# A fused attention and gated-MLP block: attention in 64x32 TensorE tiles, six score banks in turn, and one double exponential in each pair

## The chip, the cores and the metric

The kernel runs on one core of one Trainium2 chip as a single program. The core has a matrix engine (TensorE, PE below; its weight loads are PEld), a vector engine (DVE), an activation engine (ACT), a general engine (POOL) and a queue processor that issues transfers (SP). The metric is the device time of one execution in microseconds (us). Matmul results land in an accumulator memory of eight banks, each holding 128 x 512 single-precision numbers; ACT and DVE read them there. An engine takes its instructions in the order in which they stand in the program, and an instruction that needs another engine's result waits for a counter of that engine to reach a number.

## The reference, cut to what matters

```python
x = A_x                                         # [1, 2048, 512]
qkv = layernorm(x) @ wqkv                       # 32 heads of 16 columns
scores = einsum("bhqd,bhkd->bhqk", q, k) * 16 ** -0.5
p = softmax(scores); o = einsum("bhqk,bhkd->bhqd", p, v)
h = x + o @ wo
z = gelu(layernorm(h) @ w_in)                   # 1376 columns, halves z1 and z2
g = w_sp @ layernorm(z2) + b_sp[:, None]        # mixes the 2048 rows
out = h + (z1 * g) @ w_out
```

The softmax subtracts each row's maximum, so the kernel needs for each head and each of 2048 queries a bound over 2048 keys, then exp(score - bound) for all 32 x 2048 x 2048 scores, and the weighted sum of values.

## The kernel before, in words

Three stages follow each other: projections (up to about 160 us), attention (to about 1293 us), and the output projection with the gated MLP. The change lies in attention, and the rest is told only where attention meets it.

**Tiling.** Heads go in eight groups of four. Within a group the two heads t = 0 and t = 1 of a product pair sit in rows 0 to 49 and 64 to 113 of PE's array, and p = 0 or 1 chooses the pair. Queries go in four blocks of 512, keys in sixteen blocks of 128. A unit is (head group, query block, key block); the main loop takes two units, a *pair* of key blocks kb and kb1, at a time, 256 pairs in all. The split of queries and keys into half-precision parts makes the contraction 48 rows, and two rows more carry the row's bound.

**Scores and exponentials** (`score`, `product`). For each pair PE makes eight score blocks s0 to s7, each 128 keys x 512 queries with one matmul (L805) of 50 rows x 128 columns. ACT reads each from its bank and writes its exponential to a tile `pt` (L814). Three banks, three separate tiles called `s`, go round.

**Maxima for a later query block** (`max_pair`). The loop also works ahead on the bounds of a query block some pairs later. In each pair PE makes eight more products `m` (L223): seven end in a DVE pass over 128 x 512 (six `reduce_max`, L228, and one two-operand pass, L237), and one is read by ACT as an absolute value (L233) that the two-operand pass combines. Four banks, four separate tiles m0 to m3, go round. The first eleven of the 256 maxima steps run ahead of the main loop; the other 245 stand one in each of the first 245 pairs. One pair follows without maxima, and ten pairs in which a 128 x 1024 exponential over two banks takes two scores at once (`scores2`, L823), beside first matmuls of the output projection (`make_h`, L747).

**Weighted values** (`weigh`, L830). `pt` is the single-precision moving operand and 32 columns of values, one of them ones, are the stationary one: 128 rows x 32 columns, four such matmuls j = 0 to 3 side by side in the four column strips, added up in one bank `pv` over sixteen key blocks. Each is carried out as two matmul instructions. After the last key block DVE copies `pv` to `og` (`take`, L840) and two DMAs send it off; the sums come back by DMA and are inverted (`invert`, L777).

**What sets the order.** The string `PAIR` is written out by hand: the tokens s, M, H (half of the previous block's weighing), P (the whole of this block's) are emitted one after another onto the engines' queues. POOL works through a list of chores that prepare later weights, with a budget in each pair. Waits are not written in the kernel: the layer that records it sets them from the tiles that each instruction writes and reads.

Of the kernel before, what the change touches and what calls it, by code (L numbers as in the profile page):

```python
# [8 lines left out]
F32 = mybir.dt.float32  # L9
# [13 lines left out]
H = 32  # L23
# [16 lines left out]
PAIR = "s0 M0 join s2 M4 M1 s1 H s3 invert M2 s5 M3 H out M5 s4 M7 turn s6 s7 M6 P".split()  # L40
# [19 lines left out]
def block_kernel(ctx: ExitStack, tc: tile.TileContext, x, wqkv, wo, w_in, w_sp4, b_sp, w_out, out):  # L60
# [144 lines left out]
    def max_pair(m):  # L205
# [14 lines left out]
        def scores(t, keys, b):  # L220
            r = slice(RG * t, RG * t + KS)
            acc = bank(b)
            nc.tensor.matmul(acc, q[r, p, c], keys[r, p], start=True, stop=True)  # L223
            return acc

        def one(t, e, b):
            acc = scores(t, k[:, :, 512 * e:512 * e + 512], b)
            nc.vector.reduce_max(at(t, e if t else e - 1), acc, axis=AX.X)  # L228

        def minus(b):  # L230
# [4 lines left out]
        def plus(b):  # L235
# [15 lines left out]
        four = [lambda b, e=e: one(1, e, b) for e in range(4)]  # L251
        two = [lambda b, e=e: one(0, e, b) for e in (2, 3)]
# [535 lines left out]
    with ExitStack() as at:  # L788
# [4 lines left out]
        pp = at.enter_context(tc.tile_pool(name="pp", bufs=6))  # L793
        ps_v = at.enter_context(tc.tile_pool(name="ps_v", bufs=1, space=PSUM))
        inner = at.enter_context(ExitStack())
        ps_m3 = inner.enter_context(tc.tile_pool(name="ps_m3", bufs=1, space=PSUM))
        ps_s = inner.enter_context(tc.tile_pool(name="ps_s", bufs=3, space=PSUM))
        more.clear()
        more[3] = lambda: ps_m3.tile([P, 512], F32, name="m3")
        pv = {}  # L800

        def product(s, hg, qb, kb, p, t):

            r = slice(RG * t, RG * t + KM)
            nc.tensor.matmul(s, kst[hg % 2][r, p, kb * P:(kb + 1) * P],  # L805
                             qst[hg * NQ + qb][r, p, :], start=True, stop=True)

        def score(hg, qb, kb, p, t):
# [3 lines left out]
            s = ps_s.tile([P, 512], F32, name="s")  # L812
            product(s, hg, qb, kb, p, t)
            nc.scalar.activation(pts[p, kb][:, t, :], s, AF.Exp, scale=scales_[hg // 2])  # L814

        def scores2(hg, qb, kb, p):

            pts[p, kb] = pp.tile([P, 2, 512], F32, name="pt")
            turn[0] += 1
            s = later[turn[0] % 3 != 1].tile([P, 2, 512], F32, name="s2")  # L820
# [4 lines left out]
        def weigh(hg, qb, kb, a=0, b=512):  # L825
            if kb == 0:
                pv[0] = ps_v.tile([P, 512], F32, name="pv")
            for j in range(4):
                c = (4 * kb + j) * VW
                nc.tensor.matmul(pv[0][32 * j:32 * j + 32, a:b], vst[hg % 2][:, c:c + 32],  # L830
                                 pts[j % 2, kb][:, j // 2, a:b], start=kb == 0, stop=kb == NB - 1,
                                 skip_group_check=True)
            if b == 512:
                for p in range(2):
                    del pts[p, kb]

        def take(hg, qb, pool=sm):

            o = pool.tile([P, 512], F32, name="og", bufs=2)
            nc.vector.tensor_copy(o, pv[0])  # L840
# [204 lines left out]
        for n in range(0, len(units), 2):  # L1045
# [15 lines left out]
            steps = max_pair(m) if m < 8 * HG * NQ else []  # L1061
            m += 1
            if not steps and not later:
                maxima.close()
                later.append(attn.enter_context(
                    tc.tile_pool(name="ps_l", bufs=1, space=PSUM, side="right")))
                steps_h.append(make_h(h_rows[0], later[0].tile([P, 512], F32, name="h")))
            elif not steps and len(later) == 1:
                inner.close()
                later.append(at.enter_context(tc.tile_pool(name="ps_t", bufs=2, space=PSUM)))  # L1070
# [13 lines left out]
            if len(later) == 2:  # L1084
                if turned:
                    max_rows()
                more_h = n in (492, 494, 508, 510)
                scores2(hg, qb, kb, 0)
                scores2(hg, qb, kb, 1)
                some_h(1 + more_h)  # L1090
                weigh(*prev)
                if ends:
                    take(*prev[:2])
                scores2(hg, qb, kb1, 0)
                scores2(hg, qb, kb1, 1)
                some_h(1)
                weigh(hg, qb, kb)
            first = True
            for tok in PAIR if len(later) < 2 else ():
# [504 lines left out]
```

## Time and profile before

| what | value |
|---|---|
| median of 3 runs | 1713.79 us (1713.14 to 1713.97) |
| profiled execution, its span | 1712.3 us |
| median less that span | 1.5 us (the profiled execution's own time is not listed; the span and this remainder stand for it) |
| first exponential of attention | starts at 160.66 us |
| last of the 40 double exponentials | ends at 1292.5 us |
| granted PE clock, mean | 1.000 |

The page gives for each engine its busy time, that time's share of the span and its number of instructions; its slice lines give the busy share in 40 equal slices of 42.8 us, so attention fills slices 4 to 30. A group's mean duration is from the start of an instruction to its end; ACT and DVE start the next one before the end of the last, so the sum of durations can exceed the time taken. Rows of the timeline give start, duration, engine, line, operands and a count, with the idle time before it in square brackets and what ended it.

### The profile page before, as it was taken

Reading aid. Unit: us, or ns where it says so; the run is one execution under the profiler, and the core shown is the slowest. Engines: PE = TensorE matmul, PEld = TensorE weight load, DVE = VectorE, ACT = ScalarE, POOL = GpSimd, SP = SyncE. Lnnn points to the kernel's source line nnn. Section 1 sums busy time; section 2 is a strip of 40 time slices with the busy share of each in tenths; the row PEclk is TensorE's granted clock in tenths of the full one; section 3 lists DMA queues with packets and bytes.
Section 4 is the critical chain, followed back from the end, with each engine's and each line's share of the span. In section 5 each row is a group of like instructions: output and inputs, shape, how many; then the busy total and the mean of one; then the engine's idle time right before and its main releaser. Section 6 shows DMA issues by size and latency. Waiting matters only on the chain.

```text
span 1712.3 us, 36689 instructions
## 1 busy us (share of the span) xinstructions
PE 1699.5 (99%) x13508; PEld 644.7 (38%) x13508; DVE 1452.5 (85%) x3051; ACT 1317.5 (77%) x2584; POOL 813.6 (48%) x1062
## 2 busy tenths in 40 slices
PE   9999999999999999999999999999999999999999
PEld 4533222222222222222222222222225666656665
DVE  7688999999999999999999999999936787543444
ACT  4334999999999999999999999999995545211111
POOL 1231867776673267687767776400002766300100
PEclk9999999999999999999999999999999999999999
DMA  5534332342221244344434444300114454664551
GB/s 185 167 94 144 103 89 68 101 94 82 81 68 25 56 118 117 104 144 125 130 113 124 132 140 130 80 13 19 37 39 124 140 173 140 233 234 156 198 217 44
DMA packets 189309, 196.03 MB, mean 114 GB/s; under 512 B 67496, under 2 KB 140008, under 8 KB 189128
## 3 DMA queue, kind: packets, MB, share of 16 engines
q1 hardware_dynamic: 186824, 188.04, 36.8%
q10 hardware_dynamic: 2304, 5.64, 0.8%
q8 instruction: 106, 1.74, 0.4%
q14 instruction: 75, 0.61, 0.1%
HBM read 122.10 MB, written 65.93 MB: 110 GB/s over the span
## 4 chain that ended last, share of the span: by engine, by line
PE 78%; DVE 12%; DMA 3%; POOL 2%; ACT 2%; SPq 2%; issue 1%; ACTq 0%; POOLq 0%; DVEq 0%
PE pv L830 26%; PE s L805 17%; PE m L223 9%; DVE mx L228 7%; PE acc L107 4%; PE g L108 4%; PE g L109 4%; PE g L107 4%; PE acc L109 4%; PE acc L108 4%; DMA rc<-r_scr 1%; DVE ab L237 1%; DVE og L840 1%; SPq L723 1%; DVE rs_t L124 1%
## 5 line engine op out<-in xcount | busy, mean ns | idle before, releaser
L814 ACT ACTIVATE pt<-s 128x512 f32<-128x512 f32 x1968 | 1006.2, 637 | 5.5 <-PE m L223 4.3
L228 DVE TENSOR_REDUCE mx<-m 128x1 f32<-128x512 f32 x1510 | 947.5, 682 | 11.7 <-PE m L223 2.9
L805 PE MATMUL s<-qst,kst 50*128 50x512 f16 x2048 | 604.2, 379 | 0.2
L830 PE MATMUL pv<-pt,vst 128*32 128x256 f32 (+1 forms) x6056 | 598.1, 466 | 4.1 <-DVE og L840 1.3
L223 PE MATMUL m<-kst,qst 48*128 48x512 f16 x1510 | 452.4, 381 | 0.0
L805 PEld LDWEIGHTS <-kst 50*128 50x128 f16 x2048 | 132.0, 94 | 352.1 <-issue 323.7
L830 PEld LDWEIGHTS pv<-pt,vst 128*32 128x32 f32 x6056 | 119.5, 108 | 290.7 <-issue 277.3
L223 PEld LDWEIGHTS <-qst 48*128 48x128 f16 x2048 | 159.2, 93 | 173.6 <-issue 124.2
L223 PE MATMUL m<-uvs,qst 48*128 48x512 f16 x504 | 190.5, 380 | 0.6 <-DVE mx L228 0.6
L245 POOL TENSOR_SCALAR nm<-nm 128x16 f32<-128x16 f32 x32 | 6.6, 206 | 358.8 <-DVE nm L242 358.8
L237 DVE CUSTOM_DVE_ANT_0 ab<-m,ab 128x512 f32<-128x512 f32 x252 | 170.5, 677 | 2.7 <-ACT ab L233 2.7
L233 ACT ACTIVATE ab<-m 128x512 f32<-128x512 f32 x252 | 157.3, 624 | 15.5 <-PE m L223 14.8
L1368 ACT ACTIVATE pr<-pr,up 128x304 f32<-128x304 f32 (+1 forms) x32 | 17.0, 574 | 109.2 <-DVE up L1322 109.2
L991 POOL TENSOR_TENSOR op<-raw,op 128x512 f16<-128x512 f32 x80 | 92.9, 1161 | 6.0
L914 POOL TENSOR_TENSOR raw<-raw 128x512 f32<-128x512 f32 (+1 forms) x84 | 83.3, 991 | 6.7
L919 POOL TENSOR_TENSOR acc_sp<-acc_sp,raw 128x512 f32<-128x512 f32 x63 | 80.4, 1277 | 4.5
L109 PE MATMUL acc<-wi,hT 128*128 128x344 f16 x256 | 79.1, 309 | 0.3 <-DVE hT L104 0.3
L107 PE MATMUL acc<-wi,hT 128*128 128x344 f16 x256 | 79.1, 309 | 0.0
L108 PE MATMUL acc<-wi,hT 128*128 128x344 f16 x256 | 79.1, 309 | 0.0
L1510 POOL TENSOR_TENSOR pr<-pr,z 128x344 f32<-128x344 f32 x8 | 7.3, 914 | 145.9 <-DMA whole<-squares 108.3
L911 POOL TENSOR_SCALAR raw<-raw 128x512 f32<-128x512 f32 (+1 forms) x88 | 52.3, 594 | 19.7 <-DMA raw<-in_wqkv 12.4
L1509 DVE TENSOR_TENSOR pr<-g,v 128x344 f32<-128x344 f32 x8 | 4.1, 517 | 66.6 <-PE g L109 63.5
(247 smaller groups left out, 2292.9 us busy)
## 6 DMA issues: line engine op xcount, KB each, us to landing
raw<-in_w_sp SPq DMA_DIRECT2D x128, 256.0 KB
s_scr<-op SPq DMA_DIRECT2D x64, 256.0 KB
op<-s_scr SPq DMA_DIRECT2D x32, 512.0 KB
a_scr<-op SPq DMA_DIRECT2D x48, 256.0 KB
op<-a_scr SPq DMA_DIRECT2D x24, 512.0 KB
o_scr<-og SPq DMA_DIRECT2D x64, 128.0 KB
qst<-q_scr SPq DMA_DIRECT2D x192, 32.0 KB
kst<-k_scr SPq DMA_DIRECT2D x48, 128.0 KB
```

What stands on the lines that cost most here:

```text
L107: nc.tensor.matmul(ps, lh, rh, start=first, stop=False, **kw)
L108: nc.tensor.matmul(ps, lh, rl, start=False, stop=False, **kw)
L109: nc.tensor.matmul(ps, ll, rh, start=False, stop=last, **kw)
L223: nc.tensor.matmul(acc, q[r, p, c], keys[r, p], start=True, stop=True)
L228: nc.vector.reduce_max(at(t, e if t else e - 1), acc, axis=AX.X)
L233: nc.scalar.activation(ab[0], acc, AF.Abs)
L237: nc.vector.tensor_tensor_reduce(ab[0], acc, ab[0], 0.5, LOW, ALU.add, ALU.max, at(0, 0))
L805: nc.tensor.matmul(s, kst[hg % 2][r, p, kb * P:(kb + 1) * P], qst[hg * NQ + qb][r, p, :], start=True, stop=True)
L814: nc.scalar.activation(pts[p, kb][:, t, :], s, AF.Exp, scale=scales_[hg // 2])
L830: nc.tensor.matmul(pv[0][32 * j:32 * j + 32, a:b], vst[hg % 2][:, c:c + 32], pts[j % 2, kb][:, j // 2, a:b], start=kb == 0, stop=kb == NB - 1,
L914: pool.tensor_mul(got[0] if n else acc, got[0], got[0])
L991: chores.append((lambda: pool.tensor_sub(t[0][:, 1], of(), t[0][:, 0]), TT))
```

## The change

All attention matmuls of the main loop become tiles of 64 array rows x 32 array columns. A score or maxima product, one matmul before, is four (`by_quarters`, L237), one for each strip of 32 columns, with the same 512 moving columns. The weighing is split by key half: t = 0 takes keys 0 to 63 on array rows 0 to 63 and t = 1 keys 64 to 127 on rows 64 to 127, in two banks pv0 and pv1, so each weighing has twice as many matmuls with half the rows; at the end ACT copies pv1 to a tile `half` (L892) and DVE adds pv0 to it (in place of its copy).

The three `s` banks and four `m` banks become six banks of one tile, `slots`, of 128 x 6 x 512; the class `Slots` hands out the least recently used bank, or two neighbours. Scores s5 and s4 of each pair ("w5 w4") go to two neighbouring banks and one 128 x 1024 exponential (L862) takes both; the other six stay single (L851). The order strings are new: N and n are the maxima products with a `reduce_max` of head t = 1 and t = 0, A the one read by ACT (L271), C the two-operand one (L275), Q and R a half's weighing of the previous and of this key block. The first pair of a query block has a string of its own. In the last ten pairs the double exponentials draw on `slots` too, and one bank is held for the output projection.

```diff
-PAIR = "s0 M0 join s2 M4 M1 s1 H s3 invert M2 s5 M3 H out M5 s4 M7 turn s6 s7 M6 P".split()
+PAIR = "s0 s1 n N s2 Q1 Q0 s3 s6 N Q0 Q1 n w5 w4 N R0 R1 A N turn R0 s7 C R1 rows".split()
+FIRST_PAIR = "s0 s1 n N n Q1 s2 Q1 half Q0 s3 Q0 out N s6 N A w5 w4 R1 R0 R1 C turn s7 R0 N".split()
+SLOTS = 6
+    class Slots:
+        def __init__(self, pool, n):
+            self.acc = pool.tile([P, n, 512], F32, name="slots")
+            self.used, self.now = [0] * n, 0
+        def one(self):
+            i = min(range(len(self.used)), key=self.used.__getitem__)
+            self.mark(i)
+            return self.acc[:, i, :]
+        def two(self):
+            i = min(range(0, len(self.used), 2), key=lambda i: max(self.used[i:i + 2]))
+            self.mark(i)
+            self.mark(i + 1)
+            return self.acc[:, i:i + 2, :]
+    def by_quarters(acc, left, right):
+        for c in range(4):
+            c = slice(32 * c, 32 * c + 32)
+            nc.tensor.matmul(acc[c], left[:, c], right, start=True, stop=True)
         def scores(t, keys, b):
             r = slice(RG * t, RG * t + KS)
-            acc = bank(b)
-            nc.tensor.matmul(acc, q[r, p, c], keys[r, p], start=True, stop=True)
+            if slots:
+                acc = slots.one()
+                by_quarters(acc, q[r, p, c], keys[r, p])
+            else:
+                acc = bank(b)
+                nc.tensor.matmul(acc, q[r, p, c], keys[r, p], start=True, stop=True)
-        ps_m3 = inner.enter_context(tc.tile_pool(name="ps_m3", bufs=1, space=PSUM))
-        ps_s = inner.enter_context(tc.tile_pool(name="ps_s", bufs=3, space=PSUM))
+        slots = Slots(at.enter_context(tc.tile_pool(name="ps_s", bufs=1, space=PSUM)), SLOTS)
         def product(s, hg, qb, kb, p, t):
             r = slice(RG * t, RG * t + KM)
-            nc.tensor.matmul(s, kst[hg % 2][r, p, kb * P:(kb + 1) * P],
-                             qst[hg * NQ + qb][r, p, :], start=True, stop=True)
+            by_quarters(s, kst[hg % 2][r, p, kb * P:(kb + 1) * P], qst[hg * NQ + qb][r, p, :])
         def score(hg, qb, kb, p, t):
-            s = ps_s.tile([P, 512], F32, name="s")
+            s = slots.one()
+        def half_scores2(hg, qb, kb, p, t):
+            if not wide:
+                pts[p, kb] = pp.tile([P, 2, 512], F32, name="pt")
+                wide.append(slots.two())
+                product(wide[0][:, t, :], hg, qb, kb, p, t)
+            else:
+                s = wide.pop()
+                product(s[:, t, :], hg, qb, kb, p, t)
+                nc.scalar.activation(pts[p, kb], s, AF.Exp, scale=scales_[hg // 2])
-        def weigh(hg, qb, kb, a=0, b=512):
+        def weigh(hg, qb, kb, t, cols=256):
+            r, c = slice(RG * t, RG * t + RG), slice(a, a + cols)
             for j in range(4):
-                nc.tensor.matmul(pv[0][32 * j:32 * j + 32, a:b], vst[hg % 2][:, c:c + 32],
-                                 pts[j % 2, kb][:, j // 2, a:b], start=kb == 0, stop=kb == NB - 1,
-                                 skip_group_check=True)
+                v = (4 * kb + j) * VW
+                nc.tensor.matmul(pv[t][32 * j:32 * j + 32, c], vst[hg % 2][r, v:v + 32],
+                                 pts[j % 2, kb][r, j // 2, c], start=kb == 0 and not a,
+                                 stop=kb == NB - 1 and a + cols == 512,
+                                 tile_position=(RG * t, 32 * j), skip_group_check=True)
         def take(hg, qb, pool=sm):
-            nc.vector.tensor_copy(o, pv[0])
+            nc.vector.tensor_add(o, pv[0], halves.pop())
```

How the instructions of a pair stand is shown at three places, in the middle of attention, with the counters that each waits for in brackets (an engine's name with `_49` is its counter; a wait that stands alone is shown with the instruction behind it).

PE before: one matmul for each product; `m` tiles carry a number, since each bank is a tile of its own.

```order
L805 LDWEIGHTS kst_158
L805 MATMUL s<-qst,kst_158 128x512 [waits Activation_49]
L223 LDWEIGHTS qst
L223 MATMUL m_18133<-kst_1849,qst 128x512 [waits DVE_49]
L805 LDWEIGHTS kst_158
L805 MATMUL s<-qst,kst_158 128x512 [waits Activation_49]
L223 LDWEIGHTS qst
L223 MATMUL m_18140<-uvs_1850,qst 128x512 [waits DVE_49]
L830 MATMUL pv<-pt,vst_156 32x256 x4
```

PE in the changed kernel: products are rows of four with their weight loads, all into `slots`; only the first of the four waits.

```order
L237 LDWEIGHTS qst
L237 MATMUL slots<-uvs_159,qst 32x512 [waits DVE_49]
L237 LDWEIGHTS qst
L237 MATMUL slots<-uvs_159,qst 32x512
L237 LDWEIGHTS qst
L237 MATMUL slots<-uvs_159,qst 32x512
L237 LDWEIGHTS qst
L237 MATMUL slots<-uvs_159,qst 32x512
L237 LDWEIGHTS kst_158
L237 MATMUL slots<-qst,kst_158 32x512 [waits Activation_49]
```

What moved: eight instructions stand where two stood. In the rows before, the number that a product waits for is that of the instruction that last read the product's own bank, four to eight reads of a score or a maximum back. In the changed rows it is, fifteen times in a pair, that of the exponential or DVE pass that stands directly ahead in the program, of whichever bank: the product of the first row here waits for the DVE pass of the product just ahead of it, though the two lie in different banks.

ACT before, two pairs and the absolute values between them:

```order
L814 ACTIVATE pt<-s 128x512 [waits PE_49] x8
L233 ACTIVATE ab<-m_9444 128x512 [waits PE_49]
L814 ACTIVATE pt<-s 128x512 [waits PE_49] x8
L233 ACTIVATE ab<-m_9528 128x512 [waits PE_49]
L814 ACTIVATE pt<-s 128x512 [waits PE_49] x8
```

ACT in the changed kernel, one pair and the beginning of the next:

```order
L862 ACTIVATE pt<-slots 128x1024 [waits DVE_49,PE_49,Activation_49]
L271 ACTIVATE ab<-slots 128x512 [waits DVE_49,PE_49]
L851 ACTIVATE pt<-slots 128x512 [waits DVE_49,PE_49] x2
L851 ACTIVATE pt<-slots 128x512 [waits PE_49]
L851 ACTIVATE pt<-slots 128x512 [waits DVE_49,PE_49,Activation_49]
L851 ACTIVATE pt<-slots 128x512 [waits PE_49]
L851 ACTIVATE pt<-slots 128x512 [waits PE_49,Activation_49]
L862 ACTIVATE pt<-slots 128x1024 [waits DVE_49,PE_49,Activation_49]
```

What moved: two of the eight exponentials are one of 1024 columns. Before, every read of a score waits for PE alone. Now most wait for DVE's counter as well, for the DVE pass directly ahead; `Activation_49` stands for a reused `pt` buffer, several pairs back.

DVE before, the passes of one pair (the reduction of 16 columns is the negation at a block's end):

```order
L228 TENSOR_REDUCE mx<-m_11872 128x1 [waits PE_49]
L242 TENSOR_REDUCE nm<-mx 128x16 [waits DVE_49]
L228 TENSOR_REDUCE mx<-m_11885 128x1 [waits PE_49]
L228 TENSOR_REDUCE mx<-m_11888 128x1 [waits PE_49]
L228 TENSOR_REDUCE mx<-m_11901 128x1 [waits PE_49]
L228 TENSOR_REDUCE mx<-m_11916 128x1 [waits PE_49]
L228 TENSOR_REDUCE mx<-m_11922 128x1 [waits PE_49]
```

DVE in the changed kernel, one pair:

```order
L266 TENSOR_REDUCE mx<-slots 128x1 [waits PE_49,Activation_49]
L266 TENSOR_REDUCE mx<-slots 128x1 [waits PE_49]
L266 TENSOR_REDUCE mx<-slots 128x1 [waits PE_49,Activation_49]
L266 TENSOR_REDUCE mx<-slots 128x1 [waits PE_49]
L266 TENSOR_REDUCE mx<-slots 128x1 [waits PE_49,Activation_49] x2
L275 ISA ab,mx<-slots,ab 128x512 [waits PE_49,Activation_49]
L275 ISA mx 128x1
```

What moved: the same seven passes in a pair, in another order. Before, a reduction waits for PE alone; now, wherever an ACT instruction stands between two passes in the program, the second waits for ACT's counter too, for that ACT instruction.

126 lines of the change are left out of this document (66 added, 60 removed).

## The prediction

> **What bounds the kernel now.** I read the page first, its engine line and its slices, for where time lies and which engines are full there.
>
> ```profile
> span 1712.3 us, 36689 instructions
> PE 1699.5 (99%) x13508; PEld 644.7 (38%) x13508; DVE 1452.5 (85%) x3051; ACT 1317.5 (77%) x2584; POOL 813.6 (48%) x1062
> ...
> DVE  7688999999999999999999999999936787543444
> ACT  4334999999999999999999999999995545211111
> ```
>
> The change touches attention alone, about 1,130 us of the span, where three engines are full at once. One stretch of it in the view by windows says so more exactly (length; busy time and count of PE, PEld, DVE, ACT, POOL; then PE's granted clock, DMA share and GB/s):
>
> ```profile
> 750.00:1000.00 250.00, 249.12 (x2256) 70.77 (x2254) 248.14 (x479) 249.79 (x509) 182.84 (x223) 1.00 0.44 128
> ```
>
> The pace comes from ACT's rows in the timeline. The absolute value L233 stands once in a pair; its 11th and its last stand here.
>
> ```profile
> 164.29 0.60 ACT L233 ACTIVATE ab<-m 128x512 f32<-128x512 f32 x1
> ...
> 1247.96 0.62 ACT L233 ACTIVATE ab<-m 128x512 f32<-128x512 f32 x1
> 1248.44 0.63 ACT L814 ACTIVATE pt<-s 128x512 f32<-128x512 f32 x1
> ```
>
> There are 244 steps between them: (1247.96 - 164.29) / 244 = **4.44 us for a pair**. In it ACT makes nine passes, DVE seven and PE sixteen products and two weighings, and all this lies side by side: nine ACT passes of 0.64 us and seven DVE passes of 0.68, with their products, would take far longer than 4.44 one after another. What allows it is that seven banks are filled and emptied independently.
>
> ```profile
> L814 ACT ACTIVATE pt<-s 128x512 f32<-128x512 f32 x1968 | 1006.2, 637 | 5.5 <-PE m L223 4.3
> L228 DVE TENSOR_REDUCE mx<-m 128x1 f32<-128x512 f32 x1510 | 947.5, 682 | 11.7 <-PE m L223 2.9
> L805 PE MATMUL s<-qst,kst 50*128 50x512 f16 x2048 | 604.2, 379 | 0.2
> ```
>
> The idle times at the ends of these rows (5.5, 11.7 and 0.2 us) show how well that works now: hardly anyone waits.
>
> **The change part by part.** I begin with what the order of the changed kernel shows, since it decides the rest. All six banks are slices of one tile. The rows on PE show every product waiting for ACT's or DVE's counter, and the number there is that of the read directly ahead in the program, whichever bank it read. The rows on ACT show exponentials that wait for DVE, which before they never did. So a product may not start before the read of the previous product has ended, and that read can't start before its own product. Sixteen products and their readers form one chain; the banks go round, but **only one is in use at a time** (two for the double exponential).
>
> The price of a link of that chain is read where, in the trace of before, an engine stood idle and was released. First PE to reader, then reader to PE:
>
> ```profile
> 748.22 0.39 PE L805 MATMUL s<-qst,kst 50*128 50x512 f16 x1
> ...
> 748.45 0.38 PE L805 MATMUL s<-qst,kst 50*128 50x512 f16 x1
> ...
> 748.65 0.60 ACT L814 ACTIVATE pt<-s 128x512 f32<-128x512 f32 x1 [0.78 <-PE m L223]
> 748.68 0.69 DVE L228 TENSOR_REDUCE mx<-m 128x1 f32<-128x512 f32 x1
> ...
> 163.32 0.60 ACT L814 ACTIVATE pt<-s 128x512 f32<-128x512 f32 x1 [1.09 <-PE m L223]
> ...
> 163.97 0.37 PE L805 MATMUL s<-qst,kst 50*128 50x512 f16 x1
> ...
> 746.24 0.63 DVE L228 TENSOR_REDUCE mx<-m 128x1 f32<-128x512 f32 x1
> ...
> 746.92 0.37 PE L223 MATMUL m<-uvs,qst 48*128 48x512 f16 x1 [0.59 <-DVE mx L228]
> ```
>
> A product into an idle array takes 0.39 us and its reader starts 0.04 later (748.22 + 0.39 to 748.65). ACT's pass then takes 0.60, DVE's 0.69 when it starts from idle. The fourth score of a stretch starts at 163.97, 0.05 after the exponential that held its bank ended (163.92); the product at 746.92 starts 0.05 after the reduction ended (746.87).
>
> Two more passes occur, the double exponential and the two-operand one with its read-out:
>
> ```profile
> L823 ACT ACTIVATE pt<-s 128x1024 f32<-128x1024 f32 x40 | 37.6, 1021 | 0.9 <-ACT pt L814 0.3 <-PE s L805 0.2
> ...
> 747.98 0.68 DVE L237 CUSTOM_DVE_ANT_0 ab<-m,ab 128x512 f32<-128x512 f32 x1
> ...
> 748.58 0.08 DVE L237 DVE_READ_ACCUMULATOR2_ANT mx<- 128x1 f32 x1
> ```
>
> So a link costs, product + 0.04 + reader + 0.05:
> - ACT single, six exponentials and the absolute value: 0.39 + 0.04 + 0.60 + 0.05 = 1.08; seven make 7.56.
> - Double exponential, two products at once on the two array halves: 0.39 + 0.04 + 1.02 + 0.05 = 1.50. Taken alone this edit would spare one pass of ACT; in a chain it spares a whole link less 0.42.
> - DVE reduction: 0.39 + 0.04 + 0.69 + 0.05 = 1.17; six make 7.02.
> - Two-operand pass, ending with its read-out at 748.66, 0.68 after its start: 1.16.
>
> Together **17.24 us for a pair**, 12.80 more than now. 245 pairs: 3,136 us.
>
> The four small matmuls in place of one product I cost at nothing beyond this: the weighing already runs in four column strips. By form and in the timeline its rows are
>
> ```profile
> L830 PE MATMUL pv<-pt,vst 128*32 128x256 f32 x3920 | 313.1, 391 | 0.0
> ...
> 745.16 0.40 PE L830 MATMUL pv<-pt,vst 128*32 128x256 f32 x4
> ...
> 703.82 0.64 PE L830 MATMUL pv<-pt,vst 128*32 128x256 f32 x8
> ```
>
> Four of 391 ns take 0.40 us together, so four strips cost as one, and the last of a product may end 0.02 later than one alone would; sixteen times that, 0.3 us a pair, goes into the upper bound. A half's weighing of 256 columns is eight such, 0.64 us. It waits for no bank and stands in PE's queue right behind a product, where the chain has 1.08 us until the next product may start. Two halves that overlap, on different array rows as the scores of the two heads do now, need little over 0.64 and are hidden; one after the other, 1.28, they would add 0.2 to each of the four groups of a pair, 0.8. I take the first. Half's copy on ACT and the addition on DVE come once in eight pairs, on engines that are then idle more than half the time; without that cover they would cost one pass each, 1.3 us in eight pairs, 40 us in all.
>
> After the 245 pairs: one pair without maxima, 6 x 1.08 + 1.50 = 8.0 for about 4.3, adds 4. Then 40 double exponentials, which also alternate with their products now.
>
> ```profile
> 1254.34 5.87 ACT L823 ACTIVATE pt<-s 128x1024 f32<-128x1024 f32 x6 [0.26 <-ACT pt L814]
> 1260.41 32.12 ACT L823 ACTIVATE pt<-s 128x1024 f32<-128x1024 f32 x34 [0.20 <-PE s L805]
> ...
> 1262.31 0.39 PE L747 MATMUL h<-wo,o 128*128 128x512 f16 x1
> ```
>
> 38.2 us now (1254.34 to 1292.53); 40 x 1.50 = 60 then, and 24 matmuls L747 into the held bank, which is a slice of the same tile, stand in the chain with 0.2 to 0.39 each, 7 in all: 29 more. Projections and the MLP stage are not touched; POOL's chores and DMAs get more time in a pair than they need.
>
> **Sum:** span 1712.3 + 3,136 + 4 + 29 = 4,881, and with the 1.5 between span and median **4,883 us**.
>
> Bounds. Below: without any hand-over, 15 x 0.09 = 1.35 us a pair, 330 us less, 4,550. The rows above all show one, so I stay near 4,883 and go to 4,700. Above: 0.3 for strips and 0.8 for weighings a pair, 270 us, 5,150.
>
> **Rivals.**
> *The clock of PE falls.* Its mean is 1.00 in every stretch, but PE has 99% of the span there. In the chain its products stream for 0.23 us each (748.22 to 748.45, start to start) and its eight weighings for at most 8 x 0.64: under 9 of 17.24 us. If that halves the clock, each of the 15 links has 0.23 us more: 3.4 a pair, 5,710 us. For it: no stretch of the trace has so idle a PE. Against it: no pause in the chain is longer than about 0.7 us. The Trainium skill (TensorE: Matmul & The Clock Gate, Part 1) has the clock halved by an idle window of about 3.4 us; by that rule the clock stays, and no trace here has shown it yet.
>
> *The waits do not bind, and the banks work as six.* Then PE no longer drains between the 128-row weighing and the 64-row products, and DVE sets the pace. Two two-operand passes with six reductions without a gap between them:
>
> ```profile
> 272.29 0.68 DVE L237 CUSTOM_DVE_ANT_0 ab<-m,ab 128x512 f32<-128x512 f32 x1
> 272.89 0.08 DVE L237 DVE_READ_ACCUMULATOR2_ANT mx<- 128x1 f32 x1
> 272.89 3.67 DVE L228 TENSOR_REDUCE mx<-m 128x1 f32<-128x512 f32 x6
> 276.49 0.68 DVE L237 CUSTOM_DVE_ANT_0 ab<-m,ab 128x512 f32<-128x512 f32 x1
> ...
> L840 DVE COPY og<-pv 128x512 f32<-128x512 f32 x32 | 21.8, 681 | 10.2 <-PE pv L830 10.2
> ```
>
> 4.20 us, and what comes once in eight pairs, the copy L840 (0.68 / 8 = 0.09) and three small passes (taken as 0.04), make 4.33: 0.11 x 245 = 27 us less, about **1,687**, faster than before. It decides if an order on whichever bank costs nothing, as it would if each wait were long met when it is reached. Against it: the read waited for is the newest one, which by the rows cannot have ended when PE comes to the next product. The Trainium skill (Perfetto Trace Analysis, Matmuls) advises rotating independent products through different banks so that one is emptied while the next is filled; the seven banks of before agree with it (4.44 us a pair), and by that rule the time would be this rival's.
>
> *PE cannot take its instructions fast enough.* 128 matmuls and as many loads a pair, where there are 40 of each now. In 17 us that is slower than the 40 in 4.44; it could only matter in the second rival.
>
> **How the numbers follow.** The chain at full clock 0.74, own range 4,700 to 5,150. The chain at a lower clock, for some or all of the time, 0.13, from 5,150 to 5,710. Six banks that work 0.09, near 1,687. Something slower than all 0.04. The likeliest gives 4,880; the range 4,650 to 5,700 holds the first and second. A measurement of this kernel tells 0.2% from no change; faster has the third case, 0.09; the same 0.01; slower 0.90.
>
> **What would show it.** In the changed profile ACT should be busy (7 x 0.60 + 1.02) / 17.2 = 30% of attention and DVE (6 x 0.69 + 0.76) / 17.2 = 28%, with idle time ahead of nearly every L851, L266 and L271 ended by PE, and in PE's rows ahead of L237 by ACT or DVE. The rows L271 should lie 17.2 us apart. A step of 4.3 us would prove me wrong, by the second rival; steps of 20 us with a clock of 0.5, by the first. A step between 5 and 15 would mean that part of the waits is met early, and the chain is shorter than I have it.

## The result and the profile after

The changed kernel takes **5,911.4 us** (median; 5,910.2 to 5,912.6) beside 1,713.9 (1,713.1 to 1,714.4) on the same chip: 3.450 times as long, 95% interval 3.445 to 3.455. The forecast was 4,880. Slower it is, by the chain that was forecast and by a half clock to which the forecast gave a chance of 0.13.

The profiled page: the span, the engines' line, and of the forty slices those of PE, DVE, ACT and PE's granted clock.

```profile
span 5908.4 us, 82976 instructions
...
PE 3733.6 (63%) x35516; PEld 1037.2 (18%) x35516; DVE 1595.4 (27%) x3051; ACT 1526.4 (26%) x2370; POOL 810.4 (14%) x1062
...
PE   9655555555555555555555555555555555556999
...
DVE  7222222222222222222222222222222222221654
ACT  3222222222222222222222222222222222223521
...
PEclk9555555555555555555555555555555555555999
```

No engine is full from the second slice to the 37th, and the clock is 0.5 in just those slices. One stretch by windows, 600 to 1,000 us (length; busy time and count of PE, PEld, DVE, ACT, POOL; clock, DMA share, GB/s), of the kernel before and of the changed one:

```profile
600.00:1000.00 400.00, 397.98 (x3600) 112.87 (x3600) 396.20 (x766) 398.84 (x812) 289.50 (x368) 1.00 0.43 125
```

```profile
600.00:1000.00 400.00, 236.96 (x2396) 52.92 (x2396) 93.23 (x160) 98.57 (x152) 69.88 (x81) 0.50 0.07 18
```

ACT is busy 25% of the time and DVE 23%, where both had over 99%. The groups say what they waited for:

```profile
L237 PE MATMUL slots<-qst,kst 50*32 50x512 f16 x8192 | 1082.9, 596 | 974.1 <-DVE mx L266 484.1 <-ACT pt L851 322.6 <-DVE mx L275 118.6
L266 DVE TENSOR_REDUCE mx<-slots 128x1 f32<-128x512 f32 x1470 | 1017.0, 692 | 3354.6 <-PE slots L237 3350.8
...
L851 ACT ACTIVATE pt<-slots 128x512 f32<-128x512 f32 x1476 | 881.3, 597 | 2594.9 <-PE slots L237 2594.9
```

The readers wait for products and the products for readers: 3,350.8 of DVE's 3,354.6 us and all of ACT's 2,594.9 end with a product. The timeline shows links of the chain, and the rows of the absolute value L271 the step of a pair:

```profile
2000.30 0.61 PE L237 MATMUL slots<-kst,qst 48*32 48x512 f16 x4 [0.86 <-DVE mx L266]
...
2003.07 0.62 PE L237 MATMUL slots<-qst,kst 50*32 50x512 f16 x4
...
2003.73 0.60 ACT L851 ACTIVATE pt<-slots 128x512 f32<-128x512 f32 x1 [0.71 <-PE slots L237]
2004.38 0.61 PE L237 MATMUL slots<-qst,kst 50*32 50x512 f16 x4 [0.69 <-ACT pt L851]
...
2005.11 0.60 ACT L851 ACTIVATE pt<-slots 128x512 f32<-128x512 f32 x1 [0.78 <-PE slots L237]
2005.76 0.61 PE L237 MATMUL slots<-kst,qst 48*32 48x512 f16 x4 [0.76 <-ACT pt L851]
...
2010.46 0.62 PE L237 MATMUL slots<-kst,qst 48*32 48x512 f16 x4 [1.20 <-ACT pt L862]
```

```profile
L271 ACT ACTIVATE ab<-slots x245: 597/597/598, 175.8 to 5387.8; 128x512 f32<-128x512 f32 x123
```

A product takes 0.61 us where it took 0.39, its reader starts 0.66 or 0.73 after it (0.43 before), and the next product 0.05 after the reader's end: 1.31 and 1.38 us for a link. Where PE pauses between products, it is mostly for 0.7 to 0.9 us, and for 1.20 behind the double exponential L862; the longest pause of attention is 1.5. The first and the last of the 245 absolute values lie (5387.8 - 175.8) / 244 = **21.36 us a pair** apart, where 17.24 was forecast.

### The profile page after: what moved, and what is told of

Its sections match the earlier page's. It is cut to its first block, busy times and chain, and to the rows that moved or that the text cites. A ratio compares the mean times of both kernels' runs of the same rounds, so it can differ in the third digit from the quotient of the medians.

```text
span 5908.4 us, 82976 instructions
## 1 busy us (share of the span) xinstructions
PE 3733.6 (63%) x35516; PEld 1037.2 (18%) x35516; DVE 1595.4 (27%) x3051; ACT 1526.4 (26%) x2370; POOL 810.4 (14%) x1062
## 4 chain that ended last, share of the span: by engine, by line
PE 57%; ACT 20%; DVE 16%; issue 5%; DMA 1%; SPq 0%; DVEq 0%; ACTq 0%; POOL 0%; POOLq 0%
PE slots L237 39%; ACT pt L851 13%; DVE mx L266 12%; PE pv L881 11%; ACT pt L862 4%; DVE ab L275 3%; ACT ab L271 3%; PE g L110 1%; PE g L111 1%; PE g L109 1%; PE acc L109 1%; PE acc L111 1%; PE acc L110 1%; ACT pt L870 0%; DMA rc<-r_scr 0%
## 5 line engine op out<-in xcount | busy, mean ns | idle before, releaser
L266 DVE TENSOR_REDUCE mx<-slots 128x1 f32<-128x512 f32 x1470 | 1017.0, 692 | 3354.6 <-PE slots L237 3350.8
L237 PE MATMUL slots<-qst,kst 50*32 50x512 f16 x8192 | 1082.9, 596 | 974.1 <-DVE mx L266 484.1
L881 PE MATMUL pv<-pt,vst 64*32 64x256 f32 (+1 forms) x16048 | 1637.4, 636 | 0.0
L851 ACT ACTIVATE pt<-slots 128x512 f32<-128x512 f32 x1476 | 881.3, 597 | 2594.9 <-PE slots L237 2594.9
L237 PE MATMUL slots<-kst,qst 48*32 48x512 f16 x5880 | 901.7, 598 | 1014.1 <-ACT pt L851 368.5
L237 PEld LDWEIGHTS <-qst 48*32 48x32 f16 x7840 | 370.9, 100 | 2359.5 <-issue 2359.5
L237 PEld LDWEIGHTS <-kst 50*32 50x32 f16 x8192 | 324.7, 99 | 2112.4 <-issue 2111.7
L862 ACT ACTIVATE pt<-slots 128x1024 f32<-128x1024 f32 x246 | 251.9, 1024 | 817.7 <-PE slots L237 817.7
L881 PEld LDWEIGHTS pv<-pt,vst 64*32 64x32 f32 x16048 | 414.0, 142 | 134.3 <-issue 132.7
L237 PE MATMUL slots<-uvs,qst 48*32 48x512 f16 x1960 | 301.3, 598 | 178.0 <-ACT pt L851 149.4
L275 DVE CUSTOM_DVE_ANT_0 ab<-slots,ab 128x512 f32<-128x512 f32 x245 | 169.4, 692 | 574.0 <-PE slots L237 574.0
L271 ACT ACTIVATE ab<-slots 128x512 f32<-128x512 f32 x245 | 146.3, 597 | 537.1 <-PE slots L237 537.1
```

Of the source, the lines that this page charges most:

```text
L237: nc.tensor.matmul(acc[c], left[:, c], right, start=True, stop=True)
L271: nc.scalar.activation(ab[0], acc, AF.Abs)
L275: nc.vector.tensor_tensor_reduce(ab[0], acc, ab[0], 0.5, LOW, ALU.add, ALU.max, at(0, 0))
L862: nc.scalar.activation(pts[p, kb], s, AF.Exp, scale=scales_[hg // 2])
L881: nc.tensor.matmul(pv[t][32 * j:32 * j + 32, c], vst[hg % 2][r, v:v + 32], pts[j % 2, kb][r, j // 2, c], start=kb == 0 and not a, stop=kb ...
```

## The experiments

Two theories stand at the start. **The tile:** six banks in one tile are one thing to the waits, so products and readers form one chain. Rivals: the 64x32 tiles, the two sums, or the double exponential cost the time. Then, since the clock was the surprise: **why is it 0.5?** Times of the kernel before beside these runs are 1,713.3 to 1,714.0 us.

### Six tiles instead of one

All exponentials are single here, since a double one needs two banks in one tile.

```diff
-            self.acc = pool.tile([P, n, 512], F32, name="slots")
+            self.acc = [pool.tile([P, 512], F32, name=f"slot{i}") for i in range(n)]
...
-PAIR = "... n w5 w4 N R0 R1 ..."
+PAIR = "... n s5 s4 N R0 R1 ..."
```

> The changed kernel with its six banks as six tiles of their own instead of slices of one, and with all eight exponentials single (a tile of two banks would tie two banks together again). Products then wait for the read of their own bank, four to six reads back. Theory (one tile orders all reads and products one after another, and the low clock follows from the idle PE): a pair takes what ACT or DVE takes alone, 9 x 0.48 on ACT and 4.20 + 0.13 on DVE, about 4.35 us, clock 1.0, 1,690 to 1,705 us in all. Rival (the 64x32 tiles, four times the matmul instructions, are slow themselves: a product takes 0.66 us to its reader whatever the order): PE takes more than 5 us a pair, over 1,850 us, clock anywhere.

Measured: **1,744.6 us**, 1.021 times the kernel before (1.016 to 1.025). With the one tile gone, 99% of the loss is gone; the 64x32 tiles and the two sums stay in this kernel and cost about 2% together. (The double exponential went with the tile; a run below keeps it.) But it is not faster than before either. The same stretch, and ACT's rows of one pair:

```profile
600.00:1000.00 400.00, 385.90 (x11156) 209.78 (x11151) 386.04 (x742) 391.12 (x796) 279.21 (x359) 1.00 0.43 121
```

```profile
605.61 0.77 ACT L271 ACTIVATE ab<-slot 128x512 f32<-128x512 f32 x1
606.08 4.22 ACT L851 ACTIVATE pt<-slot 128x512 f32<-128x512 f32 x8
610.02 0.77 ACT L271 ACTIVATE ab<-slot 128x512 f32<-128x512 f32 x1
```

An undisturbed pair takes 4.41 us here (605.61 to 610.02), and the median step of the kernel before is 4.41 as well. In both, ACT's queue is full and its passes start 0.48 us apart (605.61 to 606.08 here, 1247.96 to 1248.44 before; 0.478 is the median of both), so nine need 4.30 us, and hold-ups of 0.02 to 0.1 us at a few passes take the rest. So ACT leaves little to win whatever the other engines do. That it alone sets the pace of the kernel before is not shown: PE and DVE are busy over 99% there too.

### The kernel before with its seven banks in one tile

The reverse: products of 128 columns, weighing, order and exponentials as before.

```diff
+        banks = ps_s.tile([P, 7, 512], F32, name="banks")
...
-        more[3] = lambda: ps_m3.tile([P, 512], F32, name="m3")
+        for i in range(4):
+            more[i] = lambda i=i: banks[:, i, :]
+        three, where = [0], [banks, 4]
...
-            s = ps_s.tile([P, 512], F32, name="s")
+            s = where[0][:, where[1] + three[0] % 3, :]
```

> The kernel before, with one thing changed: its seven score and maxima banks are slices of one tile of 128 x 7 x 512, used in the same turns as before. Products stay 128 columns wide, one instruction each, the weighing stays whole, no double exponential. Theory (the one tile makes the chain): sixteen links a pair, seven with DVE at 1.16 to 1.17 and nine with ACT at 1.08, 17.9 us at full clock and 21.6 at half, 5,000 or 5,900 us in all. Rival (tile shape or instruction count makes the time): within 2% of 1,714 us.

Measured: **6,157.9 us**. One tile alone makes the chain (22.6 us a pair: sixteen single links; 21.6, and 5,900 in all, were expected at half clock), and the clock is 0.5 here too:

```profile
600.00:1000.00 400.00, 231.66 (x708) 34.10 (x708) 88.06 (x151) 95.19 (x160) 50.71 (x62) 0.50 0.05 15
```

So neither chain nor clock comes from the 64x32 tiles or the double exponential.

### Three tiles of two banks; four of one and one of two

Both keep all else of the change, the double exponential too.

```diff
-            self.acc = pool.tile([P, n, 512], F32, name="slots")
+            self.acc = [pool.tile([P, 2, 512], F32, name=f"slots{i}") for i in range(n // 2)]
```

> The changed kernel with its six banks as three tiles of two banks each, double exponentials kept. A product now waits for the last read of its own pair of banks: about 6 of 15 products a pair wait for the read directly ahead, the others for the one four reads back or for reads between. If the ties of a tile are all that matters, the time falls in proportion to the links that are left, 6 to 9 of 15 at 1.1 us: 6.6 to 10.3 us a pair at full clock, 2,250 to 3,150 us. By (A) the clock then is 1.0 or changes between the two, since PE is busy over half of the time on two row halves; by (B) it is 0.5 since pauses between products are left, and the time is 2,600 to 3,700.

```diff
-            self.acc = pool.tile([P, n, 512], F32, name="slots")
+            self.acc = [pool.tile([P, 512], F32, name=f"slot{i}") for i in range(n - 2)]
+            self.pair = pool.tile([P, 2, 512], F32, name="slots2")
```

> The changed kernel with four tiles of one bank and one of two banks for the double exponential, as in the change. No product waits for the read directly ahead, most for the one three to five reads back. If the one tile was the whole loss, the time is near that of six separate tiles without the double exponential (1,745): 4.4 to 5.2 us a pair, 1,710 to 1,910 us, clock 1.0. If the double exponential or the 64x32 tiles cost something of their own, over 1,950.

Measured: **3,747.7 us** for three pairs, 12.7 us a pair at a clock of 0.53 in the stretch from 600 to 1,000: the order of the three is as expected, but the time is above both ranges. Counting only the products that wait for the read directly ahead was too low; what the other nine add was not taken apart. For four and one, **1,915.5 us**, 5.2 us a pair, clock 1.00: no chain, though 5 us above its range. The pair of banks that the double exponential keeps to itself leaves four for fourteen products, and DVE waits for products. That this is what makes the pair longer is likely, but it was not tried by itself:

```profile
L264 DVE TENSOR_REDUCE mx<-slot 128x1 f32<-128x512 f32 x1470 | 927.5, 684 | 140.6 <-PE slot L235 115.6 <-ACT pt L849 6.3
```

Against that, what the double exponential can save is small: two single passes of 0.48 to 0.49 (ACT's busy time over its count, 398.84 / 812, is 0.491) for one of 0.945 (the 34 in 32.12 us of the prediction's row), at most 0.04 us a pair, 9 us in all.

### What holds the clock at 0.5

The chain leaves no long pause: 1.20 us in the rows above, 1.5 at most. Four kernels add useless matmuls to the changed kernel and leave nothing out; they keep the one tile, with four slots, and write to banks that nobody reads. The first two, behind each product, repeat its four small matmuls on the same 64 rows, once and twice:

```diff
             nc.tensor.matmul(acc[c], left[:, c], right, start=True, stop=True)
+        for _ in range(FILL):
+            for c in range(4):
+                c = slice(32 * c, 32 * c + 32)
+                nc.tensor.matmul(junk[row][c], left[:, c], right, start=True, stop=True)
```

> The changed kernel, still one tile for its banks (four of them now, so that two are free), and behind each product the same four matmuls once more into a bank that nobody reads: work without use for PE, which lies beside the reader's pass. Theory (the chain, and a clock that falls because PE streams too little): the products still wait as before. If the clock goes back to 1.0 with this work, the link falls by the 0.23 us that I had at full clock: 17.2 to 18 us a pair, 4,880 to 5,100 us, although more work is done and there are fewer banks. If the clock stays at 0.5: 5,900 to 6,200 us. Rival (the small tiles are slow at any clock): the link stays near 0.66 + 0.65, 5,900 us or more, with a clock of 1.0 too.

> The same with the useless work twice behind each product, so that PE streams for most of a link. Theory: if one portion is not enough for the clock, two may be; then links at full clock with 0.21 + 0.43 of streaming, hidden but where a weighing stands behind (up to 0.4 more in four links of a pair): 17.2 to 19 us a pair, 4,880 to 5,350 us. At half the clock the useless work no longer fits beside the reader's pass everywhere: 6,000 to 7,000 us. Rival as with the single portion: 5,900 us or more at a clock of 1.0.

Measured: **6,017.5 and 6,333.0 us**. The other two use all 128 rows and columns, one and two matmuls behind each product:

```diff
             nc.tensor.matmul(acc[c], left[:, c], right, start=True, stop=True)
+        for _ in range(FULL):
+            nc.tensor.matmul(junk[1], junk[0][:, :P], junk[0], start=True, stop=True)
```

> The changed kernel with four slots in the one tile, and one useless matmul behind every product's four: all 128 rows and 128 columns of the array, 512 elements, 16 bit, into a bank of its own that nobody reads (it adds work and leaves out nothing). Two theories of why the clock fell to 0.5 in attention. (A) The clock goes by how much of the array streams in the course of time: in the chain only 64 of 128 rows work, at most some 60% of the time. Then the filler brings the clock back to 1.0, and the chain shows its price at full speed, as forecast: 17.2 to 18.5 us a pair, 4,880 to 5,250 us. (B) It goes by the short pauses that the chain leaves between products whatever streams between them. Then the clock stays at 0.5 and the time is 5,900 to 6,300 us, as for fillers on half of the rows (6,017).

> The same with two useless matmuls of the whole array behind each product. By (A) the clock is 1.0 for all of attention; product 0.39 and two fillers of 0.21 to 0.25 end 0.8 to 0.9 us after the link begins, before its reader does (1.08 to 1.17), so the time is that of one filler within 5%: 4,880 to 5,400. By (B) the clock is 0.5, and the fillers, 0.9 us at that clock, no longer fit behind the readers: 6,300 to 7,300.

Measured: **6,661.7 us** with one, above both of its ranges, and **5,461.4 us** with two, 61 above the range for a full clock: more useless work, and 1,200 us less. The same stretch of the four, in this order:

```profile
600.00:1000.00 400.00, 313.58 (x3536) 77.28 (x3528) 90.98 (x156) 96.50 (x149) 58.76 (x70) 0.50 0.06 17
```

```profile
600.00:1000.00 400.00, 371.08 (x4452) 129.25 (x4456) 86.03 (x147) 91.42 (x141) 48.04 (x56) 0.50 0.07 18
```

```profile
600.00:1000.00 400.00, 356.27 (x2371) 92.40 (x2371) 82.17 (x140) 86.06 (x133) 47.99 (x56) 0.50 0.05 15
```

```profile
600.00:1000.00 400.00, 348.99 (x3280) 109.05 (x3280) 101.88 (x174) 107.92 (x167) 70.44 (x80) 0.98 0.08 22
```

The busy share of PE doesn't tell them apart: 93% has the clock 0.50 (second), 87% has 0.98 (fourth). One more run of the first kind, with four repeats, leaves PE hardly a pause at half clock, on half of the rows:

> The changed kernel with four slots in the one tile, and each product's four small matmuls repeated four times more into a bank that nobody reads: useless work on the same 64 rows as the product, enough that PE hardly pauses even at half clock. (A) The clock goes by how much of the array streams: half of its rows all the time aren't enough, it stays at 0.5, and a link lasts as long as its five passes, 0.6 + 4 x 0.43 = 2.3 us: 35 us a pair, 8,800 to 9,600 us. (B) The clock goes by the pauses: with none left it returns to 1.0, a link is 0.39 + 4 x 0.22 = 1.3 to 1.4 us, 20 us a pair, 5,400 to 5,900 us.

Measured: **7,268.9 us**, between the two: in attention the clock is 0.5 for 3 to 106 us at a time (24 in the middle) and 1.0 between, mostly for 3 to 7 us.

```profile
600.00:1000.00 400.00, 383.06 (x5724) 180.10 (x5716) 74.09 (x127) 78.81 (x122) 46.26 (x55) 0.57 0.06 16
```

96% busy and 0.57: neither theory as it stood, but the clock seems to follow how much of the array works, not whether PE works. That can be worked out. Three fillers in a row take 0.82 us and one 0.38 (rows below), so 512 columns stream in 0.22 us at full clock. A product does that on half of the array. A weighing of 256 columns has two matmuls in each strip; four of its matmuls take 0.40 us and eight take 0.64 (rows of the prediction), so the second four add 0.24, about one more stream of 0.22, and a weighing streams for 0.44. Of a pair's time at full speed, the array's work is then, as an estimate, (16 x 0.22 + 8 x 0.44) x 0.5 = 3.5 us, and more with fillers. (The expectation of the run below counts a weighing at half of that.)

| kernel | array work, us a pair | us a pair | share | clock | PE busy |
|---|---|---|---|---|---|
| before | 3.5 | 4.44 | 79% | 1.00 | 99% |
| six tiles | 3.5 | 4.54 | 78% | 1.00 | 96% |
| four and one | 3.5 | 5.2 | 67% | 1.00 | 92% |
| two whole fillers | 10.6 | 19.4 | 54% | 0.98 | 87% |
| four half fillers | 10.6 | 26.8 | 39% | 0.57 | 96% |
| two half fillers | 7.0 | 23.0 | 31% | 0.50 | 93% |
| one whole filler | 7.0 | 24.3 | 29% | 0.50 | 89% |
| three pairs of banks | 3.5 | 12.7 | 28% | 0.53 | 68% |
| one half filler | 5.3 | 21.8 | 24% | 0.50 | 78% |
| the change | 3.5 | 21.4 | 16% | 0.50 | 59% |
| before in one tile | 3.5 | 22.6 | 16% | 0.50 | 58% |

(Clock and busy share from 600 to 1,000 us; us a pair is the mean of 244 steps, at the clock that the kernel had.) From 54% up the clock is full or nearly, up to 31% it is half or nearly, and between them it swings.

The traces' clock records allow a finer reading, since the clock changes only at multiples of 3.41 us. Attention can be cut at these marks, and the array's work in each stretch, worked out as above, set beside the clock of the next stretch. In all kernels of this document but the one with four half fillers, 9,143 stretches have a share under 38%, and 8 of them are followed by full clock; 4,243 have one over 42%, and 4 are followed by half clock. So the limit lies near 40%. PE's busy time doesn't sort them: of 2,956 stretches with PE busy 99% or more, 1,210 are followed by full clock. In the kernel with four half fillers the limit is less sharp (227 of its 524 stretches over 42% are followed by half clock); why is open. What exactly is counted, rows, columns or something that goes with them, was not varied by itself.

The Trainium skill (TensorE: Matmul & The Clock Gate, Part 1) has the clock halved by an idle window of about 3.4 us. The trace disagrees, with 0.50 for nearly all of attention and no pause of PE above 1.5 us. What the same part of the Trainium skill says of a window of fixed length agrees: the clock changes at multiples of 3.41 us.

### The chain at full clock

If the share decides, fillers placed only where the chain leaves PE idle should give the price that the prediction had for the chain alone.

```diff
+                if tok in on_pe:
+                    on_pe = on_pe[1:]
+                    FULL[0] = 0 if tok == "w5" or on_pe and on_pe[0][0] in "QR" else 3
```

> The chain as it is in the changed kernel (one tile, four slots), with useless matmuls of the whole array only where the chain leaves PE idle: three behind each product that no weighing follows (ten of sixteen a pair; none behind the first product of a double exponential), none behind the others, one in the last ten pairs. Worked out from the records of the runs so far: the clock of a stretch of 3.4 us is 1.0 when the array did about 40% or more of its full-speed work in the stretch before, 0.5 when less. A product on 64 rows streams 0.213 us on half of the array, a weighing of 256 columns the same, a filler 0.213 us on all of it: (24 x 0.5 + 30) x 0.213 = 8.9 us of a pair of 17.3, 52%. So the clock should be 1.0 through nearly all of attention, and the chain should show the price that was forecast for it at full clock: 17.2 to 18.0 us a pair, 4,880 to 5,080 us. If the clock is again 0.5, that rule is wrong: over 6,300.

Measured: **5,407.0 us**, clock 0.93 from 600 to 1,000 us, 19.2 us a pair (with 10 x 3 fillers 10.1 us of array work, 53%): the total is above what was expected, in the main since the clock still falls for 3 to 20 us at a time, behind stretches in which the array works 40% or less. But there are stretches that answer the question. One of 73 us, its windows row and its steps:

```profile
2813.00:2886.00 73.00, 60.55 (x637) 19.51 (x637) 19.74 (x34) 20.86 (x33) 0.00 (x0) 1.00 0.08 23
```

```profile
L276 ACT ACTIVATE ab<-slots x5: 597/597/598, 2813.7 to 2886.0; 128x512 f32<-128x512 f32 x5
```

(2886.0 - 2813.7) / 4 = **18.08 us a pair at full clock**, against 17.24 forecast; 18.07 is the median of this kernel's steps at full clock. Links of this kernel at full clock:

```profile
2008.67 0.38 PE L240 MATMUL junk<-fill 128*128 128x512 f16 x1
...
2008.99 0.40 PE L238 MATMUL slots<-qst,kst 50*32 50x512 f16 x4
...
2009.32 0.82 PE L240 MATMUL junk<-fill 128*128 128x512 f16 x3
2009.43 0.60 ACT L860 ACTIVATE pt<-slots 128x512 f32<-128x512 f32 x1 [0.49 <-PE slots L238]
...
2010.08 0.40 PE L238 MATMUL slots<-kst,qst 48*32 48x512 f16 x4
...
2010.59 0.69 DVE L271 TENSOR_REDUCE mx<-slots 128x1 f32<-128x512 f32 x1 [2.62 <-PE slots L238]
...
2011.34 0.40 PE L238 MATMUL slots<-kst,qst 48*32 48x512 f16 x4
...
2011.78 0.69 DVE L271 TENSOR_REDUCE mx<-slots 128x1 f32<-128x512 f32 x1 [0.49 <-PE slots L238]
...
2012.53 0.40 PE L238 MATMUL slots<-kst,qst 48*32 48x512 f16 x4
...
2012.54 0.64 PE L890 MATMUL pv<-pt,vst 64*32 64x256 f32 x8
...
2012.97 0.69 DVE L271 TENSOR_REDUCE mx<-slots 128x1 f32<-128x512 f32 x1 [0.50 <-PE slots L238]
2013.71 0.40 PE L238 MATMUL slots<-qst,kst 50*32 50x512 f16 x4 [0.53 <-DVE mx L271]
```

ACT's link is 1.09 (2008.99 to 2010.08; forecast 1.08). A reduction behind another reduction is 1.19 (2011.34 to 2012.53; forecast 1.17), but one behind an exponential 1.26 (2010.08 to 2011.34): its reader starts 0.51 after the product, not 0.44. In the changed kernel it is so with 8 of the 15 readers of a pair, 0.72 to 0.77 after the product instead of 0.66, and their records carry ACT's counter beside PE's; the others don't. That ACT's counter in the wait makes the 0.07 is what fits, it was not tried by itself.

### Parts of the change that were costed at nothing

The strips alone, in the kernel before:

```diff
-            nc.tensor.matmul(acc, q[r, p, c], keys[r, p], start=True, stop=True)
+            by_quarters(acc, q[r, p, c], keys[r, p])
...
-            nc.tensor.matmul(s, kst[hg % 2][r, p, kb * P:(kb + 1) * P],
-                             qst[hg * NQ + qb][r, p, :], start=True, stop=True)
+            by_quarters(s, kst[hg % 2][r, p, kb * P:(kb + 1) * P], qst[hg * NQ + qb][r, p, :])
```

> The kernel before with one part of the change alone: each product as four matmuls of 32 columns instead of one of 128; seven separate banks, weighing, order and exponentials as before. The prediction cost the strips at nothing: 1,710 to 1,720 us. If strips cost what the upper bound allowed, 0.3 us a pair (or if the array takes longer to change between 64x32 and 128x32 tiles), 1,760 to 1,800.

Measured: **1,729.0 us**, 1.009 times before (1.007 to 1.011). Neither was right: strips cost 0.06 us a pair (4.50 for 4.44), where PE has no time left (397.96 of 400 us busy in the usual stretch), a fifth of the bound of 0.3.

What the six separate tiles lack against the kernel before, 31 us, was looked for in the maxima's rows, on which PE was seen to wait:

```diff
-PAIR = "s0 s1 n N s2 ... C R1 rows".split()
+PAIR = "s0 s1 rows n N s2 ... C R1".split()
```

> The changed kernel with six separate one-bank tiles and single exponentials, as in the run with 1,745 us, and two words of the order moved: the end of the maxima of eight pairs ('rows') stands near the start of the next pair as it did before, not at its end. If the 31 us that six separate tiles lacked against the kernel before are mainly PE's waits for the maxima's rows from DRAM, which land a pair too late, they go: 1,720 to 1,728, and what stays is 0.32 us at each change of block of eight pairs. If they are strips, weighings or banks, nothing changes: 1,740 to 1,750.

Measured: **1,745.1 us**, no change; this theory fell. PE's waits for those rows, 3.6 us in all with six tiles, are gone from its table of waits; what leads it now was mostly there before (waited for: us in total, times, longest):

```profile
PE slot L237 <- DVE mx L266: 8.6, 36, 1.1
PE pv L881 <- issue: 6.9, 9, 1.3
PE slot L237 <- issue: 2.3, 4, 0.8
```

About 9 us lie at the changes of block: a block of eight pairs that nothing else disturbs takes 35.8 us, in the kernel before 35.5, and there are thirty. Most of the rest are pairs with a pause of about 1 us, some of them on PE with nothing shown that ends it ("issue"). Why is open. None of these kernels is faster than the kernel before.

## Why the prediction was wrong

**The chain was right.** That every product waits for the read directly ahead, that one bank is in use at a time, and that the readers' idle time ends with a product: shown by the groups above, and by the two runs that take the one tile away (1,745) and add it to the kernel before (6,158).

**The step that failed** is the one that took the clock to stay at 1.0: "Against it: no pause in the chain is longer than about 0.7 us." Most pauses are nearly as short as that (0.7 to 0.9 us, once in a pair 1.2), and the clock fell all the same, for nearly all of attention, as the first rival had it with a chance of only 0.13. The prediction argued from the pauses of PE and from its busy time; what the runs follow is the share of the array that works, 16% in the chain and 79% before, with a limit near 40%. Both shares could have been worked out from the rows at hand, though where the limit lies could not. The size of that rival was right: 21.36 - 18.08 = 3.28 us a pair beside its 3.4 (the 18.08 in a kernel with fillers).

**The sum at full clock** was 0.84 us a pair too low: 18.08 for 17.24, 206 us in all, within the bounds given for the chain (4,883 + 206 = 5,089, in 4,700 to 5,150). The term mis-sized is the step from a product to its reader, taken as 0.43 for every link: it is 0.44 for about half of them and 0.50 to 0.55 for the other eight, which makes some 0.75 of the 0.84; the rest is hundredths elsewhere.

The sum again, with measured terms: 4,883 + 206 + 245 x 3.28 (804) = 5,893, of 5,911. (The two new terms together are the measured step, so this tests only what is left.) The ends of attention hold the remaining 18 and more: the changed kernel runs 520.5 us after its last absolute value (5,387.8 of 5,908.4) where the one before ran 464.3 (1,248.0 of 1,712.3), 56 more, and 33 were forecast.

**The second rival** (six banks that work, 1,687) was not reached with the waits gone either: six tiles take 1,745, and four and one 1,915.5. Neither is its kernel, since a double exponential needs two banks in one tile. It took DVE for the pace, at 4.33 us; ACT's nine passes, 0.478 apart, need 4.30. So even without its chain, this change had little to win: 0.14 of 4.44 us a pair, 34 us in all, and at most 9 more by the double exponential.

**Strips and weighings** costed at nothing beside the chain: the weighings are hidden at full clock (a link of a reduction is 1.19 without one, 2011.34 to 2012.53, and 1.18 with one behind its product, 2012.53 to 2013.71). The strips' 0.06 us a pair shows only where PE is full.

**What would show it:** ACT's 25% and DVE's 23% in attention (30 and 28 forecast) are the forecast busy time over a longer pair; steps of 21.4 us with a clock of 0.5 were named for the first rival.

## What to carry to other kernels

Banks that should be filled and emptied independently must be separate tiles wherever waits are made from tiles: look which read each product's wait names, and if it is the newest one, the banks are one bank. When a change makes PE wait, price its clock as well, by the part of the array that works in the course of time and not by the pauses or PE's busy share. Before buying time on one engine, read from the timeline how far apart each engine's passes start when its queue is full: that, times their number, is the least that a step can take, and it caps the gain, here from 4.44 to 4.30 us.

## What the runs showed of the hardware

- The clock stood at 0.50 with PE busy 93% and 89% of the time, and at 0.98 with 87%: by estimate the first two worked the array to about 30%, the last to 54%. Two useless matmuls of the whole array behind each product made a kernel 1,200 us faster than one did.
- The clock changes at multiples of 3.41 us, and follows the work of the array in the 3.41 us before, by the estimate above: under 38% all but 8 of 9,143 such stretches are followed by half clock, over 42% all but 4 of 4,243 by full (one kernel left out, in which the limit is less sharp). Near the limit it swings: with four half fillers 0.5 for 3 to 106 us, then 1.0, mostly for 3 to 7.
- ACT passes over 128x512 from a full queue start 0.48 us apart, though one alone lasts 0.60 from start to end.
